# Attention and two MLPs on one core: block pairs, weight conversion and query transposes moved

## The chip, the cores and the metric

The kernel runs on one core of one Trainium2 chip. The metric is the device time of one execution in microseconds (us); a time is the median over runs. The core has five engines that run their own instruction streams in order and wait for each other by semaphores: TensorE (PE in the profile, its weight loads PEld), VectorE (DVE), ScalarE (ACT), GpSimd (POOL) and SyncE (SP), which here issues nearly all DMAs.

## The reference

Three stages, all in float32, over 4608 tokens (8 batches of 576) of width 512 (8 heads of 64):

```python
# attention, per batch and head
q_s = exp(q - max(q, -1)); q_s /= sum(q_s, -1) + 1e-09      # softmax over the 64 features
k_s = exp(k - max(k, seq)); k_s /= sum(k_s, seq) + 1e-09    # softmax over the 576 tokens
kv  = einsum('bhsd,bhse->bhde', k_s, v)
x   = einsum('bhsd,bhde->bhse', q_s, kv)                    # then (4608, 512)
# first MLP: w_in 512 x 2048, w_out 2048 x 512
h = x @ w_in;  y = (h * clip(h + 3, 0, 6) / 6) @ w_out
# second MLP, the same shapes
h = y @ w2_in; out = (h * sigmoid(h)) @ w2_out
```

## The kernel before

Tokens go in 9 blocks of 512 (`NB`). A matmul operand in float32 is held as a high part and a rest, both in the matmul's own rounded format (`F32R`), and each product is three matmuls of 128x128 weights on 512 columns (high by high, high by rest, rest by high). Weights are converted to this form by bit operations (`Conv`: `scale` and `scale_low` on ACT; `shift`, `round`, `sign` on DVE; `upper` on ACT; `lower` on DVE or POOL).

A block can be done in two ways. In the **plain** way (`mm1`, `gate`, `mm2`), a block takes 16 steps of 24 matmuls, 384 in all. In the **pair** way two blocks are multiplied together by a scheme of 7 instead of 8 products of half-size blocks (Strassen's in Winograd's form). A pair is one *pass*, with an inner half (input weights; `inner`, eight rounds `n` of the products P1, P6, P5, P2, P7, P3 and, two slots into the next round, P4) and an outer half (output weights; `outer`, 56 products). Each product is one slot of 6 matmuls, so a pass is 112 slots and 672 matmuls. It needs sums of weight parts, split into high part and rest, which lie in DRAM (`ws`), and it reads them through a ring of six buffers, two parts a fetch.

The program runs in this order:

- `first_block()` (to about 140 us): the attention of block 0 and part of the following ones, conversion of the first MLP's weights, and block 0 of the first MLP in the plain way.
- `middle()` (to about 716 us): plain blocks 1 to 6 of the first MLP (`NCL` is 7 plain blocks with block 0), and beside them the attention for the blocks to come, in *units* `u` of one block and two heads; the conversion of the second MLP's weights (`Parts`, 16 of them: 8 of `w2_in`, then 8 of `w2_out`), and the weight sums of the first MLP (`Resident`). A planner (`Plan`) writes out the order on each engine from assumed durations, keys (`begin`, `WORK`, `FETCH`, in steps) and counts of buffers.
- `second_mlp()`: five passes in the order of `PASSES`: (1, 1), (0, 7), (1, 3), (1, 5), (1, 7), where the first number is the MLP and the second the first block of the pair; then block 0 of the second MLP in the plain way. Here the order on each engine is that of the slot times given to `when`, sorted. A pass starts at slot 112 b.

In a unit of the attention, POOL and DVE normalize the queries into the one buffer `qe`. Units up to `DIRECT` (9, so all up to block 2's first) are then turned by four TensorE transposes (`q_turn`, line 476) and copied out by ACT (`q_copy`). Later units are turned by DVE in 32x32 blocks (`q_blocks`, line 484), stored to DRAM and loaded back in the right order (`q_store`, `q_load`, five DMAs).

Steps that the prediction follows in the code: in `pair_events`, `u2` and `u3` are DVE sums that read a PSUM bank before P7 and P4 may add to it, and `s5` is ACT's copy before P3; `t1` and `t2` are POOL differences of two gate outputs; `split` and `split_low` (lines 1469 to 1475) make the high part and the rest of an operand of `outer` four slots (`LOOK`) before its use; `x_ahead` makes the next pass's input operands in the outer half; `joins` adds up the results. `add` (line 1352) is the helper that records sums under line 1353.

Of the kernel before, what the change touches and what calls it, by code (L numbers as in the profile page):

```python
# [18 lines left out]
P = 128  # L19
# [9 lines left out]
def efficient_attention_then_two_mlps(  # L29
# [42 lines left out]
    ident = const.tile([P, P], F32, name="ident")  # L72
    minus = att.tile([P, DM], F32R, tag="sp", bufs=3, name="minus")[:, 0:P]
    peaks = const.tile([P, P], F32, name="peaks")
    kvt = [const.tile([P, P], F32, name=f"kv{i}") for i in range(KVS)]
# [95 lines left out]
    NPR = NF // 2  # L171
    HALF = DM // 2
# [844 lines left out]
    def middle():  # L1017

        DIRECT = 2 * NP + 1
# [5 lines left out]
        n_k, n_q, n_v, qsub, ksub, kvmm, xmm, vlow, xready = ({} for _ in range(9))  # L1025
# [4 lines left out]
        def unit(u):  # L1030
# [20 lines left out]
            if has_k and not old:  # L1051
                km = add(
                    "DVE", 1.1, key(0), lambda: k_max(u), [n_k.get(u)], ["m1", "t2k"], ["t2k"], True
# [12 lines left out]
            if has_k:  # L1066
# [3 lines left out]
                    [kx, n_v.get(u), xmm.get(u - 1)], ["a"], ["ke"],  # L1070
                )
                va = add("DVE", 0.45, key(4), lambda: kv_sum(u), [mm])
                vlow[u] = add("ACT", 0.55, key(4), lambda: kv_scale(u), [va], [], ["a"])
# [12 lines left out]
            xs_ = dma(0.35, key(6), lambda: x_store(u), 256, [xc], [], ["t2k"])  # L1086
            if j < NCL:
# [17 lines left out]
        for k in range(2 * NPR):  # L1105
            o, i = divmod(k, NPR)
            at = NF + 5.5 * k + 6 + WORK[k]
            p, done = Parts(i, o), []
            for n, c in enumerate(p.conv):
# [11 lines left out]
            for m, fn in enumerate(p.total):  # L1121
                done = [add("POOL", 0.68, at + 1.3, fn, done, [], [], True)]
            for n in range(2):
# [104 lines left out]
    def raw_x(to, j, h):  # L1228
        nc.sync.dma_start(to, yd[j, 2 * h : 2 * h + 2].rearrange("c p n -> p c n"))
# [35 lines left out]
    def first_operands():  # L1265

        def start():
            op["spare"] = xs.tile([P, 8, BLK], F32, tag="x", name="spare")
            x_steps(1)["b12"]()
# [7 lines left out]
        def load(name):  # L1277
            def do():
                operand(name, 1)
                x_steps(1)[name.lower()]()  # L1280
# [7 lines left out]
        for n, name in enumerate(("B22", "B11", "B21")):  # L1288
            jobs.append((name.lower(), "SP", 0.35, 2.5 + n, load(name), 512, ("r1",), ["wi"], False))

        def total(name, key, deps):
            jobs.append((name, "POOL", 2.1, key, lambda: x_steps(1)[name](), 0, deps, [], True))
# [42 lines left out]
    def second_mlp(last):  # L1335
        fixed = []
        for t in (kbuf[0], vbuf[0], kbuf[1], vbuf[1]):
            flat = t.rearrange("p a b c -> p (a b c)")
            fixed.append(flat[:, 0:BLK])
        for _ in range(2):  # L1340
            t = raw.tile([P, 2, BLK], F32, tag="raw", name="fin")
            fixed += [t[:, 0], t[:, 1]]
# [218 lines left out]

        turned = []
# [26 lines left out]
        def turn_last(j, k):  # L1589
# [11 lines left out]
            for i in range(4):  # L1601
# [4 lines left out]
                )  # L1606

# [140 lines left out]
```

## Time and profile before

| | |
|---|---|
| time, median of 3 runs | 1572.56 us (1572.24 to 1572.74) |
| the profiled execution: its time, its span | 1573.41 us, 1571.7 us |
| PE busy | 1557.0 us, 99% of the span, 7403 matmuls |
| DVE, ACT, POOL busy | 71%, 48%, 31% |
| TensorE clock granted | full from the first slices on |
| DMA | 342.81 MB, mean 218 GB/s |

How to read the profile: times are from one execution taken by the hardware profiler. Busy time is the union of an engine's instructions, so an instruction's own duration (mean ns) is longer than the time it takes from its engine's stream where instructions overlap. L559 is line 559 of the kernel. "<-" separates what is written from what is read; an idle time is put down to what ended it.

### The profile page before, as it was taken

The numbers are of one execution on the slowest core, as the hardware profiler recorded it, in microseconds if no ns is written. First come the engines' busy times: TensorE is split into PE (matmuls) and PEld (weight loads), VectorE is DVE, ScalarE is ACT, GpSimd is POOL, SyncE is SP. The second block draws the span as 40 slices with busy tenths as digits, with TensorE's granted clock in tenths as the row PEclk, the third lists the DMA queues.
The fourth block names the chain that finished last, engine by engine and source line by source line (L and its number), as shares of the span: only waits on it lengthen the run. The fifth ranks groups of instructions, "written<-read, shape, count | busy, mean of one in ns | idle before, by whom it ended". The sixth has DMA issues, their size and how long they took to land.

```text
span 1571.7 us, 22243 instructions
## 1 busy us (share of the span) xinstructions
PE 1557.0 (99%) x7403; PEld 1272.4 (81%) x7403; DVE 1115.9 (71%) x1791; ACT 761.0 (48%) x1358; POOL 489.2 (31%) x446
## 2 busy tenths in 40 slices
PE   7999999999999999999999999999999999999999
PEld 4787878888888888888888888888888888888887
DVE  7989577776777776555689569856976797677732
ACT  6887345554555544443365236533643464345422
POOL 4334224433434335421232242234223422440000
PEclk9999999999999999999999999999999999999999
DMA  9915976776786855746566786765668875879850
GB/s 280 335 44 176 334 227 209 238 231 203 226 257 212 264 193 189 234 152 208 189 223 217 209 233 219 260 206 198 228 213 213 224 247 194 227 224 372 260 129 27
DMA packets 346226, 342.81 MB, mean 218 GB/s; under 512 B 126464, under 2 KB 252160, under 8 KB 346112
## 3 DMA queue, kind: packets, MB, share of 16 engines
q1 hardware_dynamic: 344496, 340.70, 68.3%
q8 instruction: 59, 0.97, 0.3%
q10 hardware_dynamic: 1616, 0.69, 0.2%
q14 instruction: 55, 0.45, 0.1%
HBM read 247.20 MB, written 94.11 MB: 217 GB/s over the span
## 4 chain that ended last, share of the span: by engine, by line
PE 95%; DVE 2%; ACT 1%; DMA 1%; POOL 1%; issue 0%; SPq 0%; DVEq 0%; ACTq 0%; POOLq 0%
PE pb L1366 24%; PE pb L1525 24%; PE h L559 21%; PE y L634 19%; PE y L636 3%; PE pa L513 2%; PE pa L412 1%; DVE fa L140 0%; PE pa L384 0%; DMA ahead<-in_q_dram 0%; DMA qraw<-in_q_dram 0%; DMA wi_early<-in_moe_w_in_dram 0%; PE pa L476 0%; PE busy L875 0%; PE pa L372 0%
## 5 line engine op out<-in xcount | busy, mean ns | idle before, releaser
L559 PE MATMUL h<-x,wi 128*128 128x512 f32 x1536 | 381.8, 396 | 2.0 <-POOL wi L165 0.9
L1366 PE MATMUL pb<-xo,ring 128*128 128x512 f32 x1680 | 383.0, 389 | 0.0
L1525 PE MATMUL pb<-gsp,ring 128*128 128x512 f32 x1680 | 382.4, 389 | 0.0
L1366 PEld LDWEIGHTS pb<-xo,ring 128*128 128x128 f32 x1680 | 315.3, 188 | 65.9 <-issue 0.5
L1525 PEld LDWEIGHTS pb<-gsp,ring 128*128 128x128 f32 x1680 | 315.3, 188 | 65.5
L559 PEld LDWEIGHTS h<-x,wi 128*128 128x128 f32 x1536 | 283.2, 188 | 65.2 <-POOL wi L165 1.9
L634 PE MATMUL y<-g,wo 128*128 128x512 f32 x1344 | 323.6, 390 | 0.0
L634 PEld LDWEIGHTS y<-g,wo 128*128 128x128 f32 x1344 | 251.3, 188 | 52.7
L1353 DVE TENSOR_TENSOR gsp<-g,gsp 128x512 fp32r<-128x512 f32 x240 | 184.4, 788 | 25.0 <-ACT gsp L1471 24.2
L1471 ACT CAST gsp<-g 128x512 fp32r<-128x512 f32 x240 | 143.6, 622 | 105.4 <-PE pb L1525 89.1
L599 DVE SCALAR_TENSOR_TENSOR h<-r,h 128x512 f32<-128x512 f32 x112 | 77.7, 693 | 108.4 <-ACT r L572 108.2
L572 ACT ACTIVATE r<-h 128x512 f32<-128x512 f32 x112 | 66.9, 597 | 175.1 <-PE h L559 173.2
L1353 POOL TENSOR_TENSOR xst<-xst 128x512 f32<-128x512 f32 x32 | 70.8, 2212 | 168.6 <-DVE xo L1353 84.5
L1353 DVE TENSOR_TENSOR g<-r,pb 128x512 f32<-128x512 f32 x96 | 65.7, 684 | 54.6 <-ACT r L1380 54.1
L1380 ACT ACTIVATE r<-pb 128x512 f32<-128x512 f32 x96 | 57.1, 595 | 97.2 <-DVE pb L1353 72.8
L1353 POOL TENSOR_TENSOR g<-g 128x512 f32<-128x512 f32 x40 | 53.5, 1337 | 148.6 <-DVE g L1353 123.4
L1353 POOL TENSOR_TENSOR s<-U,s 128x512 f32<-128x512 f32 x32 | 42.6, 1330 | 173.3 <-DVE U L1353 173.3
L590 ACT CAST g<-h 128x512 fp32r<-128x512 f32 x112 | 65.5, 585 | 48.8 <-DVE h L599 40.6
L593 DVE TENSOR_TENSOR g<-h,g 128x512 fp32r<-128x512 f32 x97 | 66.8, 689 | 28.6 <-ACT g L590 26.5
L1353 DVE TENSOR_TENSOR U<-pb,s 128x512 f32<-128x512 f32 x80 | 55.0, 688 | 17.0 <-PE pb L1366 12.5
L195 POOL TENSOR_TENSOR fa<-fa 128x256 f32<-128x256 f32 x64 | 49.9, 780 | 40.7 <-DVE sp L227 32.2
L1380 ACT ACTIVATE r<-s 128x512 f32<-128x512 f32 x32 | 20.2, 632 | 87.3 <-POOL s L1353 70.3
(160 smaller groups left out, 1751.4 us busy)
## 6 DMA issues: line engine op xcount, KB each, us to landing
ring<-ws SPq DMA_DIRECT2D x280, 512.0 KB, 3.9
ws<-sp SPq DMA_DIRECT2D x128, 256.0 KB, 3.2
wi_early<-in_moe_w_in_dram SPq DMA_DIRECT2D x16, 512.0 KB, 8.5
wo_early<-in_moe_w_out_dram SPq DMA_DIRECT2D x16, 512.0 KB, 9.2
wi_raw<-in_moe_w_in_dram SPq DMA_DIRECT2D x16, 512.0 KB, 4.7
ws<-w_sum SPq DMA_DIRECT2D x32, 256.0 KB, 3.1
ws<-fa SPq DMA_DIRECT2D x32, 256.0 KB, 2.8
wo_raw<-in_moe_w_out_dram SPq DMA_DIRECT2D x16, 512.0 KB, 4.4
```

Of the source, the lines that this page charges most:

```text
L195: lambda to=to, x=x, y=y, op=op: nc.gpsimd.tensor_tensor(out=at[to], in0=at[x], in1=at[y], op=op)
L559: nc.tensor.matmul(h, w[:, a, c, :], x[:, e, c, :], start=(c == 0 and n == 0), stop=(c == NC - 1 and n == 2),)
L572: nc.scalar.activation(self.r, self.h, AF.Relu, bias=3.0)
L590: nc.scalar.copy(self.g[:, 0], self.r)
L593: nc.vector.tensor_tensor(out=self.g[:, 1], in0=self.r, in1=f32(self.g[:, 0]), op=ALU.subtract)
L599: nc.vector.scalar_tensor_tensor(out=self.h, in0=self.r, scalar=6.0, in1=self.h, op0=ALU.min, op1=ALU.mult)
L634: nc.tensor.matmul(y[c], w[:, a, cs], g[:, e, :], start=st, stop=sp)
L1353: (eng or nc.vector).tensor_tensor(out=out, in0=a, in1=b, op=how)
L1366: nc.tensor.matmul(to, ws_[:, a], e[:, c], start=p in ("P1", "P6", "P5") and c == 0 and m == 0, stop=c == 1 and m == 2, skip_group_check=True,
L1380: nc.scalar.activation(r, d[b, n, key], AF.Sigmoid)
L1471: nc.scalar.copy(t[0], source(p, i))
L1525: nc.tensor.matmul(d[b, p][m], w[:, a, m * P : (m + 1) * P], t[e], start=new and i == 0 and k == 0, stop=i == NPR - 1 and k == 2, skip_gro ...
```

## The change

Blocks 5 and 6 join blocks 7 and 8 of the first MLP as a pair (`NCL` 5 instead of 7), and both pairs are the first passes. The middle has four plain blocks instead of six, and its keys are drawn together. The eight `Parts` of `w2_out` leave the middle (`PARTS` is 8) and are made by a new function, `late_part`, inside the inner halves of the first three passes; it has the same operations as `Parts` but for POOL, in buffers that are free there. All queries are turned by TensorE (`DIRECT` 36 instead of 9). The first pass's input operands come from the attention's store `xq` instead of the first MLP's `yd`. The key-value buffers become six, and small constants are laid into common tiles.

```diff
-    KVS = NP + 1
-    NCL = NB - 2
+    KVS = NP + 2
+    NCL = NB - 4
-    PASSES = ((1, 1), (0, NCL)) + tuple((1, j) for j in range(3, NB, 2))
+    PASSES = ((0, NCL), (0, NCL + 2)) + tuple((1, j) for j in range(1, NB, 2))
...
+    PARTS = 2 * NPR - 8
...
-        m2 = tmp.tile([P, 8, D], F32, tag="t2k", name="m2")[:, 0:4]
-        m2 = m2.rearrange("p (h a) d -> p h a d", h=2)
+        m2 = halved.rearrange("p (h j d) -> p h j d", h=2, j=2)
...
-            begin[j * NP + pr] = 3 * pr if j == 1 else NF - 3 + int(3.3 * n) + LATE[n]
+            begin[j * NP + pr] = 3 * pr if j == 1 else NF - 3 + int(2.0 * n) + LATE[n]
...
-        DIRECT = 2 * NP + 1
+        DIRECT = NB * NP
...
-                qt_ = add("PE", 0.65, key(3), lambda: q_turn(u), [qn], ["a"], ["qe"])
-                ql = add("ACT", 0.62, key(3), lambda: q_copy(u), [qt_], ["qT"], ["a"])
+                qt_ = add("PE", 0.65, key(3), lambda: q_turn(u), [qn], ["a", "qT"], ["qe"])
+                ql = add("ACT", 0.62, key(3), lambda: q_copy(u), [qt_], [], ["a"])
...
-            at = NF + 5.5 * k + 6 + WORK[k]
+            at = NF + 3.4 * k + 6 + WORK[k]
-            for n, c in enumerate(p.conv):
+            for n, c in enumerate(p.conv if k < PARTS else ()):
...
-                m = None
+                m = free.get(n - 1)
...
-        nc.sync.dma_start(to, yd[j, 2 * h : 2 * h + 2].rearrange("c p n -> p c n"))
+        nc.sync.dma_start(to, xq[j - FAR, 2 * h : 2 * h + 2].rearrange("c p n -> p c n"))
...
+        words = [
+            t.rearrange("p a n -> p (a n)").bitcast(U32).rearrange("p (f t) -> p f t", t=2) for t in fin[::-1]
+        ]
+        sums = [[basis, kvs[:, 0:BLK]], [v0, kvs[:, 0:BLK]]]
+        pieces = [(kvs[:, BLK : 2 * BLK], k1), (v1, k0)]
+
+        def late_part(i, t, odd):
+            a = sums[odd]
+            rows = [2 * i, 2 * i + 1]
+            def load(n):
+                nc.sync.dma_start(
+                    words[n].rearrange("p f t -> p (f t)"),
+                    w_src[1][1][rows[n] * P : (rows[n] + 1) * P, :].bitcast(U32),
+                )
+            def scale(n):
+                nc.scalar.mul(a[n], words[n][:, :, 1].bitcast(F32), 2.0**-112)
+                nc.scalar.mul(words[n][:, :, 0], words[n][:, :, 0], 2.0**-29)
+            def bits(n):
+                au = a[n].bitcast(U32)
+                nc.vector.tensor_scalar(
+                    out=au, in0=au, scalar1=3, scalar2=None, op0=ALU.logical_shift_left
+                )
+                nc.vector.tensor_tensor(out=au, in0=au, in1=words[n][:, :, 0], op=ALU.add)
+                nc.vector.scalar_tensor_tensor(
+                    out=au, in0=words[n][:, :, 1], scalar=0x80000000, in1=au,
+                    op0=ALU.bitwise_and, op1=ALU.bitwise_or,
+                )
+            def upper(n):
+                nc.scalar.copy(pieces[n][0].bitcast(F32R), a[n])
+            def lower(n, keep):
+                hi, lo = pieces[n]
+                add((lo if keep else a[n]).bitcast(F32R), a[n], hi, ALU.subtract)
+            def store(n, keep):
+                part = Split(1, 1, i, None, NAMES[1][n] if keep else [INTO[x] for x in NAMES[1][n]], keep)
+                part.hi, part.lo = pieces[n][0], pieces[n][1] if keep else a[n]
+                part.store()
+            total = sums_in_place(1, a)
+            for n in range(2):
+                when(t - 7 + 2 * n, lambda n=n: load(n))
+                when(t + 2.2 * n, lambda n=n: scale(n))
+                when(t + 1 + 2.4 * n, lambda n=n: bits(n))
+                for k, at in enumerate((t + 3.2 + 2 * n, t + 11 + 0.6 * n)):
+                    when(at, lambda n=n: upper(n))
+                    when(at + 1 + 0.2 * k * n, lambda n=n, k=k: lower(n, not k))
+                    when(at + 2.2 + 0.2 * k * n, lambda n=n, k=k: store(n, not k))
+            for m in range(4):
+                when(t + 7.6 + 0.7 * m, total[m])
...
+        for i, t in enumerate((9, 29, 49, 121, 141, 161, 233, 250)):
+            late_part(i, t, i % 2)
```

## Rows read from the trace of the kernel before

**Rows 1.** The page, part 1: busy time, share of the span, instructions.
```profile
PE 1557.0 (99%) x7403; PEld 1272.4 (81%) x7403; DVE 1115.9 (71%) x1791; ACT 761.0 (48%) x1358; POOL 489.2 (31%) x446
```

**Rows 2.** The page, part 4: the chain that ended last, by engine.
```profile
PE 95%; DVE 2%; ACT 1%; DMA 1%; POOL 1%; issue 0%; SPq 0%; DVEq 0%; ACTq 0%; POOLq 0%
```

**Rows 3.** The page, part 5: matmuls of a plain block and of the inner halves.
```profile
L559 PE MATMUL h<-x,wi 128*128 128x512 f32 x1536 | 381.8, 396 | 2.0 <-POOL wi L165 0.9
L1366 PE MATMUL pb<-xo,ring 128*128 128x512 f32 x1680 | 383.0, 389 | 0.0
L634 PE MATMUL y<-g,wo 128*128 128x512 f32 x1344 | 323.6, 390 | 0.0
```

**Rows 4.** Stretches: length, busy PE, PEld, DVE, ACT, POOL, clock, DMA share, GB/s.
```profile
28.70:140.00 111.30, 108.16 (x543) 84.38 (x544) 101.33 (x182) 94.70 (x177) 36.83 (x32) 1.00 0.53 174
140.00:716.00 576.00, 575.33 (x2966) 469.25 (x2964) 396.92 (x688) 279.27 (x506) 221.65 (x245) 1.00 0.71 226
1071.30:1080.80 9.50, 9.50 (x43) 7.88 (x42) 5.44 (x8) 3.32 (x7) 3.87 (x3) 1.00 0.61 208
1090.30:1099.90 9.60, 9.60 (x44) 7.93 (x43) 7.33 (x11) 5.09 (x10) 3.34 (x3) 1.00 0.65 209
1099.90:1109.40 9.50, 9.50 (x44) 7.86 (x43) 9.35 (x14) 6.58 (x12) 4.64 (x4) 1.00 0.70 260
1405.00:1481.00 76.00, 76.00 (x337) 62.94 (x336) 58.09 (x87) 39.69 (x65) 3.70 (x3) 1.00 0.92 324
```

**Rows 5.** The chain in order of time: an unbroken stretch of matmuls.
```profile
796.74 74.80 PE pb L1525 x330
```

**Rows 6.** PE's timeline around one query transpose in the first block.
```profile
109.98 0.60 PE L476 MATMUL pa<-ident,qe 128*128 128x128 f32 x4
110.34 1.64 PE L559 MATMUL h<-x,wi 128*128 128x512 f32 x6
111.82 2.00 PE L634 MATMUL y<-g,wo 128*128 128x512 f32 x8
```

**Rows 7.** What PE waited for, total, times, longest: the query transposes.
```profile
PE pa L476 <- POOL qe L468: 0.5, 2, 0.3
```

**Rows 8.** Groups of DVE instructions: busy us, mean ns, idle time before.
```profile
L599 DVE SCALAR_TENSOR_TENSOR h<-r,h 128x512 f32<-128x512 f32 x112 | 77.7, 693 | 108.4 <-ACT r L572 108.2
L593 DVE TENSOR_TENSOR g<-h,g 128x512 fp32r<-128x512 f32 x97 | 66.8, 689 | 28.6 <-ACT g L590 26.5 <-PE y L634 0.7
L133 DVE TENSOR_SCALAR fa<-fa 128x512 uint32<-128x512 uint32 x64 | 35.5, 555 | 2.0 <-ACT fa L121 1.9
L140 DVE CUSTOM_DVE_ANT_0 fa<-fa,fr 128x1024 uint16<-128x1024 uint16 x64 | 51.4, 804 | 3.3
L144 DVE SCALAR_TENSOR_TENSOR fa<-wo_raw,fa 128x512 uint32<-128x512 uint32 x16 | 12.6, 790 | 0.3
L227 DVE TENSOR_TENSOR fa<-fa,sp 128x512 fp32r<-128x512 f32 x32 | 23.7, 747 | 0.6 <-ACT sp L224 0.6
L484 DVE STREAM_TRANSPOSE qz<-qe 128x512 f32<-128x512 f32 x27 | 19.0, 704 | 0.7 <-POOL qe L468 0.7
```

**Rows 9.** DVE's timeline at the end of the third pass's inner half.
```profile
1091.96 0.69 DVE L1353 TENSOR_TENSOR U<-pb,s 128x512 f32<-128x512 f32 x1
1093.86 1.35 DVE L1353 TENSOR_TENSOR gsp<-g,gsp 128x512 fp32r<-128x512 f32 x1
1097.11 0.69 DVE L1353 TENSOR_TENSOR gsp<-g,gsp 128x512 fp32r<-128x512 f32 x1 [1.30 <-ACT gsp L1471]
1098.32 0.68 DVE L1353 TENSOR_TENSOR U<-pb,s 128x512 f32<-128x512 f32 x1
```

**Rows 10.** POOL's timeline in the same stretch.
```profile
1092.01 1.29 POOL L1353 TENSOR_TENSOR g<-g 128x512 f32<-128x512 f32 x1 [2.06 <-DVE g L1353]
1093.37 1.29 POOL L1353 TENSOR_TENSOR spare<-g,g 128x512 f32<-128x512 f32 x1
```

**Rows 11.** PE's timeline there: the last round's P4.
```profile
1099.85 1.52 PE L1366 MATMUL pb<-xo,ring 128*128 128x512 f32 x6
```

More of the change, by code (lines that the diff above doesn't have):

```diff
@@ L70, in efficient_attention_then_two_mlps @@
     ps_a = ctx.enter_context(tc.tile_pool(name="ps_a", bufs=2, space=PSUM))
-    ident = const.tile([P, P], F32, name="ident")
+    basis = const.tile([P, 4 * P], F32, name="basis")
+    ident, peaks, halved = basis[:, 0:P], basis[:, P : 2 * P], basis[:, 2 * P :]
     minus = att.tile([P, DM], F32R, tag="sp", bufs=3, name="minus")[:, 0:P]
-    peaks = const.tile([P, P], F32, name="peaks")
-    kvt = [const.tile([P, P], F32, name=f"kv{i}") for i in range(KVS)]
+    kvs = const.tile([P, 2 * BLK], F32, name="kvs")
+    kvt = [kvs[:, i * P : (i + 1) * P] for i in range(KVS)]
     vbufs = const.tile([P, 2, KCH + 1, 2, D + 1], F32, name="vbuf")
@@ L1024, in middle @@
         add = plan.add
-        n_k, n_q, n_v, qsub, ksub, kvmm, xmm, vlow, xready = ({} for _ in range(9))
+        n_k, n_q, n_v, qsub, ksub, kvmm, xmm, vlow, xready, xstored = ({} for _ in range(10))
         def dma(us, key, fn, kb, deps=(), take=(), give=()):
@@ L1052, in unit @@
                 km = add(
-                    "DVE", 1.1, key(0), lambda: k_max(u), [n_k.get(u)], ["m1", "t2k"], ["t2k"], True
+                    "DVE", 1.1, key(0), lambda: k_max(u), [n_k.get(u)], ["m1"]
                 )
@@ L1069, in unit @@
                     "PE", 0.48, key(4), lambda: kv_mm(u, a_pool),
-                    [kx, n_v.get(u), xmm.get(u - 1)], ["a"], ["ke"],
+                    [kx, n_v.get(u)], ["a"], ["ke"],
                 )
-                va = add("DVE", 0.45, key(4), lambda: kv_sum(u), [mm])
-                vlow[u] = add("ACT", 0.55, key(4), lambda: kv_scale(u), [va], [], ["a"])
+                va = add("DVE", 0.45, key(4), lambda: kv_sum(u), [mm, vlow.get(u - 2)])
+                vlow[u] = add("ACT", 0.55, key(4), lambda: kv_scale(u), [va, xmm.get(u - KVS + NP)], [], ["a"])
             xm = xmm[u] = add(
@@ L1086, in unit @@
             xs_ = dma(0.35, key(6), lambda: x_store(u), 256, [xc], [], ["t2k"])
+            xstored[j, pr] = xs_
             if j < NCL:
@@ L1120, in middle @@
                 done.append(parted(p.split[n], at + n + 0.2, [c3]))
-            for m, fn in enumerate(p.total):
+            for m, fn in enumerate(p.total if k < PARTS else ()):
                 done = [add("POOL", 0.68, at + 1.3, fn, done, [], [], True)]
-            for n in range(2):
+            for n in range(2 if k < PARTS else 0):
                 parted(p.split[2 + n], at + 1.4 + n, done, ["t2k"])
@@ L1181, in middle @@
             deps = [pair_at[d] for d in deps] + [free[base + int(key)]]
+            if at[0] == "b":
+                deps += [xstored[NCL + int(at[2]) - 1, 2 * int(at[1]) - 2 + n] for n in range(2)]
             if eng == "SP":
@@ L1268, in start @@
             op["spare"] = xs.tile([P, 8, BLK], F32, tag="x", name="spare")
[L1269 removed]
+            x_steps(NCL)["b12"]()
         def get(f):
@@ L1279, in do @@
                 operand(name, 1)
-                x_steps(1)[name.lower()]()
+                x_steps(NCL)[name.lower()]()
             return do
@@ L1288, in first_operands @@
         for n, name in enumerate(("B22", "B11", "B21")):
-            jobs.append((name.lower(), "SP", 0.35, 2.5 + n, load(name), 512, ("r1",), ["wi"], False))
+            jobs.append((name.lower(), "SP", 0.35, 2.5 + n, load(name), 512, ("r1", "b12"), ["wi"], False))
         def total(name, key, deps):
-            jobs.append((name, "POOL", 2.1, key, lambda: x_steps(1)[name](), 0, deps, [], True))
+            jobs.append((name, "POOL", 2.1, key, lambda: x_steps(NCL)[name](), 0, deps, [], True))
         def split(name, key, deps):
@@ L1335, in second_mlp @@
     def second_mlp(last):
[L1336 to L1342, printed above, removed]
+        k0, v0, k1, v1 = (
+            t.rearrange("p a b c -> p (a b c)")[:, 0:BLK] for t in (kbuf[0], vbuf[0], kbuf[1], vbuf[1])
+        )
+        fin = [raw.tile([P, 2, BLK], F32, tag="raw", name="fin") for _ in range(2)]
+        fixed = [
+            x for m, (one, three) in enumerate(((k0, k1), (v0, v1)))
+            for x in (one, fin[0][:, m], three, fin[1][:, m])
+        ]
         whole = xs.tile([P, 4, 2, DM], F32R, tag="x", name="ring")
```

5 lines of the change are left out of this document (3 added, 2 removed).

## The prediction, made before the run

> **What bounds the kernel now.** I read the page's busy times first, then the chain, then the stretches, then the places where the change puts work. TensorE is busy for 99% of the span [rows 1], and the chain that ended last is 95% PE [rows 2]. The reader should see that nothing else sets the end: between 140 and 716 us, where the change takes out two blocks, PE idles 0.67 us of 576 although DVE is busy for 69% of it [rows 4]. Only the first block shows idle time, 3.14 us of 111.3, with DVE at 91% [rows 4]. So the time changes by what PE's own stream loses and gains, plus any wait that the change newly puts on PE. DVE's load matters only as a source of such waits.
>
> The unit price is that of one matmul in an unbroken stretch: 330 of them take 74.80 us, 0.2267 us each, and a slot of six 1.36 us [rows 5]. The durations of 389 to 396 ns in [rows 3] overlap and are not a price.
>
> **The pair.** A plain block has 192 matmuls at line 559 and 192 at line 634: 1536 and 1344 are eight and seven times 192, the eighth being the second MLP's plain block [rows 3]. A pass has 1680/5 = 336 inner and as many outer [rows 3], so 672. Two plain blocks have 768. The change takes away 96 matmuls: 96 x 0.2267 = **21.8 us off**. This is certain as far as the counts go. The order of the passes costs PE nothing by itself: blocks 5 and 6 reach `xq` from the attention about seven steps before the first pass reads them by the keys, and the pass with blocks 1 and 2 now comes third.
>
> **The query transposes.** 27 units get four TensorE transposes each. In the first block they begin at 109.98 and the next matmul at 110.34, so the four take 0.36 us of starts; the six matmuls behind take 1.48 us instead of 1.36, since the weights after a transpose load late [rows 6]. One unit alone costs 0.36 + 0.12 = 0.48 us. Where the transposes stand next to other attention work that late load is paid already, so 0.36 is the lower bound. I take 0.44, because both cases occur: 27 x 0.44 = **11.9 us added** (9.7 to 13.0). What they replace lay on no path: 27 DVE transposes, 19.0 us [rows 8], and 135 DMAs on SP's queue. The 27 copies by ACT go beside; ACT is busy for 48% of the middle [rows 4].
>
> A page of the Trainium skill would make this part a loss. "TensorE: Matmul & The Clock Gate", Part 4, gives about 275 ns for a transpose in a kernel; 27 x 4 x 0.275 is an estimate of 29.7 us, and the change would come out near 1588.6 us. The trace decides: four of them take 0.36 to 0.48 us together here [rows 6].
>
> **The shorter middle.** It loses 32 steps (174.1 us) and gains 11.9, so 414 us remain of 576. DVE loses 32 x (0.69 + 0.69) = 44 us of gates, 16 conversions of 0.56 + 0.80 + 0.79 + 2 x 0.75 = 3.65 us, 58 us, and the 19.0 us of transposes [rows 8]: 397 - 121 = 276 us, or 67% of the new length against 69%. Attention and `w2_in` lie mostly in the first two thirds, so DVE is nearer to the first block's 91% there than the mean says. Moving the keys together shortens each unit's distance to the next; buffers `qe` and `qT` are single, and `q_turn` must now wait for `qT` until the former unit's `x_mm` has run. Behind a PE instruction that waits stand all later matmuls, so a late query stops PE, which a late DVE transpose did not. Row: nine units cost 0.5 us of waiting for POOL's normalization [rows 7]; 27 give 1.5. Bounds: nothing (the old middle), and the first block's idle rate over 414 us, 3.14/111.3 x 414 = 11.7 us [rows 4]. I take **1.5 us added**, nearer to the old middle, whose mean DVE load is the new one's.
>
> **The late weights in the passes.** Each of the eight late parts puts on DVE two times `bits` (0.56 + 0.80 + 0.79) and four rests of 0.75, 7.3 us in all [rows 8], within 14 slots (19 us). A round of an inner half is 7 slots, and DVE is busy for 5.44 of its 9.5 us [rows 4], so two rounds leave 8.1 us. Parts that begin at slot 9, 26 or 29 of a pass fit: **0.6 us** for the six (0 to 3). ACT has more room, 3.32 of 9.5 us busy [rows 4]. In DMA a part brings 1 MB in and 2 MB out within 20 slots, 27 us, some 115 GB/s on top of 208; the last outer half moved 324 GB/s while PE was unbroken [rows 4], so I cost it at nothing. Its cover is the ring, twelve slots ahead; SP's stores wait for DVE's rests, and the fetches behind them wait too.
>
> The parts at slot 49 of the first and second pass (t = 49 and 161) do not fit. Their first DVE work falls into slots 50 to 56, where DVE also makes the first operands of the outer half: 7.33 of 9.6 us busy, 2.3 idle [rows 4]. Ahead of the last round's `u3` stand both `bits` and one rest, 5.05 us, so `u3` is 2.75 us late. It ended at 1099.00 and P4 began at 1099.85 [rows 9, 11]: the slack is 0.85, and PE waits 1.9 us. The next slice has 0.15 us of DVE idle [rows 4], so the other three rests, 2.2 us, are passed on; operands made four slots ahead absorb perhaps half, and 1.1 us is left. A tail costs 3.0 us, bounds 1.0 (most of it absorbed) and 4.9 (7.3 less all idle time). Two tails: **6.0 us added** (2 to 9.8).
>
> POOL makes this worse. A DVE rest that met POOL's `t2` took 1.35 us and ended 0.5 us after it; the one 3 us later took 0.69 [rows 9, 10]. A late part's DVE work meets `t1` and `t2` in the same way. The Trainium skill, "SBUF — State Buffer", section "Who interferes with whom", says that a DVE instruction with two SBUF inputs and a GpSimd one that reads SBUF lock each other out for the whole instruction; that speaks against work placed here, and the trace agrees. Without such a lock I should put a tail at 1.8 instead of 3.0 us and the whole 2.4 us lower.
>
> **Sum.** -21.8 + 11.9 + 1.5 + 0.6 + 6.0 = -1.8 us. Against the profiled execution (1573.41 us, span 1571.7, 1.7 us outside) that is 1571.6; this execution is 0.85 us over the median, and the median 1572.56 gives **1570.8 us**. A measurement can tell 0.2% here, 3.1 us, so the forecast is no measurable change; its own range, from the tails' 4 to 8 us and the middle's 0 to 3, is 1567 to 1574.
>
> **Rivals.**
> - *The cover holds.* Tails and middle together cost up to 5 us. For it: `outer` makes its operands four slots ahead, and in slots 56 to 63 DVE already runs at 98% without stopping PE [rows 4]. Against it: `u3` has 0.85 us of slack and no such lead. -9.9 + (0 to 5) gives 1562.7 to 1567.7.
> - *The middle becomes DVE's.* Queries and keys reach PE late at the first block's rate from the first unit on: 11.7 us, in all -9.9 + 6.6 + 11.7 = +8.4, 1581.0 us. It decides as soon as all waits exceed 13 us. For it: the packed first two thirds and single `qe` and `qT`. Against it: the old middle waited 0.67 us.
> - *The ring starves* in the first inner halves. The late traffic comes in bursts, with the stores blocking SP; a wait of 2 to 4 us in each of the first two passes gives about 1577. Against it: 324 GB/s with PE unbroken [rows 4].
> - *The transposes do not overlap* with what follows and cost their whole 0.60 us [rows 6]: 16.2 instead of 11.9, 1575.1 us; the page cited above points there. The start times speak against it.
>
> **How the numbers follow.** Forecast 0.42, cover holds 0.33, middle 0.17, ring 0.05, transposes 0.03. About a fifth of the forecast's cases lie under 1569.4 and count as faster: 0.33 + 0.08 = 0.41 faster; 0.36 the same, with a few mild cases of the rivals; the rest slower, 0.23. The range leaves out the far ends of the first two rivals: 1563 to 1580.
>
> **What would show it.** Matmuls at lines of the inner and outer halves must be 2016 each, and PE's busy time falls by about 10 us. Right: PE's idle time after 28 us grows by some 8 us, of which the greater part is P4 waiting for `u3`, and the outer half's first products waiting for DVE rests, in passes one and two near their slots 50 to 66; the third pass shows none. The query transposes wait 1 to 2 us for POOL in all. Wrong: unbroken matmuls through both places (the cover holds), idle time spread over the middle before PE's attention work (the middle), or matmuls waiting for ring fetches. A transposed unit that costs over 0.5 us would make the second term wrong.

## The result, and the profile after

The changed kernel takes **1591.05 us** (median of 4 runs, 1589.22 to 1591.73), the kernel before 1572.52 beside it: ratio 1.0116, interval 1.0099 to 1.0134. It is 18.5 us slower, and the forecast of 1570.8 us with its range of 1563 to 1580 missed it. The profiled execution of after took 1589.22 us, 1.8 us under its median, with a span of 1587.0 us; the sums below are made against the span of before, 1571.7 us, which leaves 15.3 us to explain (the execution of before lay 0.9 us over its median).

The page of after, part 1 (answers [rows 1]) and the matmul groups of part 5 (answers [rows 3]; us busy, mean ns, idle time before the group):

```profile
PE 1557.7 (98%) x7415; PEld 1263.1 (80%) x7415; DVE 1183.1 (75%) x1849; ACT 799.7 (50%) x1433; POOL 549.8 (35%) x478
...
L1370 PE MATMUL pb<-xo,ring 128*128 128x512 f32 x2016 | 463.8, 390 | 11.8 <-ACT s L1410 6.4
L1529 PE MATMUL pb<-gsp,ring 128*128 128x512 f32 x2016 | 462.1, 390 | 2.7 <-DVE gsp L1357 2.5
L559 PE MATMUL h<-x,wi 128*128 128x512 f32 x1152 | 293.9, 399 | 1.8 <-POOL wi L166 0.9
L634 PE MATMUL y<-g,wo 128*128 128x512 f32 x960 | 235.0, 393 | 0.0
```

The counts are those foreseen: 2016 matmuls in the inner halves and as many in the outer. What is new is the third column: the inner halves had no idle time ahead of their matmuls before, now 11.8 us, and the outer halves now have 2.7.

What PE waited for in after (total us, times, longest), the lines that concern the change:

```profile
PE pb L1370 <- ACT s L1410: 6.4, 5, 2.3
PE pb L1370 <- DVE U L1357: 5.1, 4, 1.5
PE pb L1529 <- DVE gsp L1357: 2.5, 4, 0.9
PE pa L384 <- ACT kvs L429: 1.8, 1, 1.8
PE pa L513 <- DVE ke L393: 1.0, 1, 1.0
PE pa L476 <- POOL qe L468: 0.8, 3, 0.3
```

L1410 is `s5`, ACT's copy ahead of P3; `U` at L1357 is `u2` or `u3` on DVE, ahead of P7 and P4; `gsp` is the rest of an operand of the outer half.

The end of the middle and the first four passes of after (stretch, length, busy PE, PEld, DVE, ACT, POOL, clock, DMA share, GB/s):

```profile
422.00:556.60 134.60, 134.60 (x657) 108.53 (x657) 84.45 (x128) 68.35 (x118) 65.82 (x66) 1.00 0.53 176
556.60:719.00 162.40, 158.11 (x685) 127.60 (x684) 137.51 (x201) 84.31 (x150) 51.89 (x36) 1.00 0.81 275
719.00:882.20 163.20, 156.57 (x674) 125.10 (x673) 134.54 (x191) 82.71 (x148) 62.41 (x44) 1.00 0.79 264
882.20:1039.00 156.80, 153.23 (x674) 125.89 (x673) 128.51 (x181) 79.67 (x141) 57.70 (x40) 1.00 0.73 245
1039.00:1191.30 152.30, 152.30 (x674) 126.11 (x673) 116.34 (x169) 69.68 (x124) 49.96 (x32) 1.00 0.74 221
```

The fourth pass is unbroken, 152.3 us, 672 x 0.2267. The three passes with late parts take 162.4, 163.2 and 156.8 us. The first contains 2.7 us of other matmuls; by the starts of PE's matmuls the rest over 152.3 us is 7.4, 10.8 and 4.5 us, 22.6 in all, and comes from waiting. With these starts the span's 15.3 us divide so:

| | predicted us | read in after |
|---|---|---|
| two plain blocks replaced by a pass | -21.8 | -21.8 (32 steps of 5.44, a pass of 152.3) |
| 27 query transposes | +11.9 | +12.4 (27 x 0.46) |
| waits in the middle | +1.5 | +2.3 |
| late parts at slots 9, 26, 29 | +0.6 | +9.7 |
| late parts at slot 49, two tails | +6.0 | +13.0 (5.9 and 7.1) |
| a wait in the first pass of before, now gone | 0 | -0.4 |
| sum | -1.8 | +15.2 |

The two terms of the late parts are the sums, slot by slot, of what the starts of six matmuls are apart beyond 6 x 0.2267 us. Tails are slots 53 to 70; the early parts show at P3 of rounds 2 and 4 above all. What a wait costs in starts is more than the idle time that the profile shows for it: the 2.26 us of idle time in the next section cost 2.5 us, because idle time counts from the end of the matmul before (0.39 us long) and not from the start that was due 0.23 us behind it, and because the second matmul after the wait comes 0.11 us late as well. Of the 22.6 us only 14.5 (11.8 and 2.7) are listed as idle. In what follows "waits" of whole passes are counted by the starts, and single waits ahead of one product by idle time unless the text says otherwise.

**How one wait comes about.** The third pass has no tail, and its longest wait, ahead of round 4's P3, is 2.26 us. PE, ACT, DVE and POOL there in after (start, us, engine, line, operation):

```profile
931.38 1.89 PE L1370 MATMUL pb<-xo,ring 128*128 128x512 f32 x7 [2.26 <-ACT s L1410]
...
930.26 0.60 ACT L1384 ACTIVATE r<-pb 128x512 f32<-128x512 f32 x1 [3.39 <-DVE pb L1357]
930.75 0.58 ACT L1410 COPY s<-pb 128x512 f32<-128x512 f32 x1
...
925.39 0.69 DVE L1357 TENSOR_TENSOR U<-pb,s 128x512 f32<-128x512 f32 x1
925.99 1.14 DVE L1589 TENSOR_SCALAR kvs<-kvs 128x512 uint32<-128x512 uint32 x1
927.26 1.57 DVE L1592 CUSTOM_DVE_ANT_0 kvs<-fin,kvs 128x1024 uint16<-128x1024 uint16 x1
928.87 0.69 DVE L1593 SCALAR_TENSOR_TENSOR kvs<-fin,kvs 128x512 uint32<-128x512 uint32 x1
929.48 0.69 DVE L1357 TENSOR_TENSOR pb<-s,pb 128x512 f32<-128x512 f32 x1
...
925.56 1.30 POOL L1357 TENSOR_TENSOR g<-g 128x512 f32<-128x512 f32 x1 [3.38 <-DVE g L1357]
926.93 1.35 POOL L1357 TENSOR_TENSOR spare<-g,g 128x512 f32<-128x512 f32 x1
```

Read it upwards. POOL makes `t1` and `t2` from 925.56 to 928.28. Beside them the late part's shift takes 1.14 us and its round 1.57, each ending 0.3 to 0.55 us after a POOL operation; sign, behind both, takes 0.69. So the three end 3.5 us after `u2`, where undisturbed they take 1.8. Only then comes `c21` (929.48), then ACT's activation of the former round, which waits for it, and behind that, on ACT's in-order stream, `s5`. PE's P3 waits for `s5`. The wait is named after ACT, ACT had idled 3.39 us, and the cause is on DVE and POOL.

**The tail.** DVE, POOL, ACT and PE of the second pass of after, at the end of its inner half:

```profile
792.56 1.58 DVE L1592 CUSTOM_DVE_ANT_0 vbuf<-fin,vbuf 128x1024 uint16<-128x1024 uint16 x1
794.17 1.66 DVE L1593 SCALAR_TENSOR_TENSOR vbuf<-fin,vbuf 128x512 uint32<-128x512 uint32 x1
795.76 0.68 DVE L1357 TENSOR_TENSOR U<-pb,s 128x512 f32<-128x512 f32 x1
...
809.13 1.63 POOL L1357 TENSOR_TENSOR spare<-g,g 128x512 f32<-128x512 f32 x1
810.72 1.19 POOL L197 TENSOR_TENSOR vbuf<-vbuf 128x256 f32<-128x256 f32 x1
811.98 1.07 POOL L197 TENSOR_TENSOR vbuf<-kvs,vbuf 128x256 f32<-128x256 f32 x1
...
813.09 0.62 ACT L1599 CAST kvs<-vbuf 128x512 fp32r<-128x512 f32 x1 [2.87 <-POOL vbuf L197]
...
796.49 3.42 PE L1370 MATMUL pb<-xo,ring 128*128 128x512 f32 x12 [1.54 <-DVE U L1357]
802.70 1.65 PE L1370 MATMUL pb<-xo,ring 128*128 128x512 f32 x6 [1.43 <-DVE U L1357]
815.71 9.12 PE L1529 MATMUL pb<-gsp,ring 128*128 128x512 f32 x36 [0.93 <-DVE gsp L1357]
```

P7 waits for `u2` behind round and sign, P4 for `u3`, and the outer half's slot 64 for a rest. The last comes by a way that the prediction didn't have: POOL makes most of the part's totals (L197) only after `t2`, ACT's `upper` (L1599) waits 2.87 us for them, and ACT's high parts of the outer operands stand behind it.

### The profile page after: what moved, and what is told of

Read it like the earlier page. It is cut to its first block, busy times and chain, and to the rows that moved or that the text cites. A ratio compares the mean times of both kernels' runs of the same rounds, so it can differ in the third digit from the quotient of the medians.

```text
span 1587.0 us, 22379 instructions
## 1 busy us (share of the span) xinstructions
PE 1557.7 (98%) x7415; PEld 1263.1 (80%) x7415; DVE 1183.1 (75%) x1849; ACT 799.7 (50%) x1433; POOL 549.8 (35%) x478
## 5 line engine op out<-in xcount | busy, mean ns | idle before, releaser
L1370 PE MATMUL pb<-xo,ring 128*128 128x512 f32 x2016 | 463.8, 390 | 11.8 <-ACT s L1410 6.4
L1529 PE MATMUL pb<-gsp,ring 128*128 128x512 f32 x2016 | 462.1, 390 | 2.7 <-DVE gsp L1357 2.5
L1370 PEld LDWEIGHTS pb<-xo,ring 128*128 128x128 f32 x2016 | 377.0, 188 | 96.7 <-ACT s L1410 10.7
L1529 PEld LDWEIGHTS pb<-gsp,ring 128*128 128x128 f32 x2016 | 377.7, 188 | 85.2 <-DVE gsp L1357 6.1
L559 PE MATMUL h<-x,wi 128*128 128x512 f32 x1152 | 293.9, 399 | 1.8 <-POOL wi L166 0.9
L559 PEld LDWEIGHTS h<-x,wi 128*128 128x128 f32 x1152 | 210.8, 188 | 48.2 <-POOL wi L166 1.9
L1357 DVE TENSOR_TENSOR gsp<-g,gsp 128x512 fp32r<-128x512 f32 x288 | 222.9, 792 | 25.8 <-ACT gsp L1475 25.1
L634 PE MATMUL y<-g,wo 128*128 128x512 f32 x960 | 235.0, 393 | 0.0
L634 PEld LDWEIGHTS y<-g,wo 128*128 128x128 f32 x960 | 178.5, 188 | 37.2
L1357 POOL TENSOR_TENSOR xst<-xst 128x512 f32<-128x512 f32 x40 | 92.7, 2318 | 202.1 <-DVE xo L1357 114.0
L1357 POOL TENSOR_TENSOR s<-U,s 128x512 f32<-128x512 f32 x40 | 53.7, 1341 | 207.1 <-DVE U L1357 199.6
L1357 POOL TENSOR_TENSOR g<-g 128x512 f32<-128x512 f32 x48 | 65.6, 1367 | 154.7 <-DVE g L1393 87.5
L1357 DVE TENSOR_TENSOR g<-r,pb 128x512 f32<-128x512 f32 x96 | 65.6, 683 | 44.8 <-ACT r L1384 43.8
L1357 DVE TENSOR_TENSOR U<-pb,s 128x512 f32<-128x512 f32 x96 | 65.8, 686 | 14.3 <-PE pb L1370 10.7
L1357 POOL TENSOR_TENSOR spare<-g,g 128x512 f32<-128x512 f32 x48 | 66.2, 1379 | 3.8
```

The lines of the kernel that those rows point to most:

```text
L559: nc.tensor.matmul(h, w[:, a, c, :], x[:, e, c, :], start=(c == 0 and n == 0), stop=(c == NC - 1 and n == 2),)
L634: nc.tensor.matmul(y[c], w[:, a, cs], g[:, e, :], start=st, stop=sp)
L1357: (eng or nc.vector).tensor_tensor(out=out, in0=a, in1=b, op=how)
L1370: nc.tensor.matmul(to, ws_[:, a], e[:, c], start=p in ("P1", "P6", "P5") and c == 0 and m == 0, stop=c == 1 and m == 2, skip_group_check=True,
L1529: nc.tensor.matmul(d[b, p][m], w[:, a, m * P : (m + 1) * P], t[e], start=new and i == 0 and k == 0, stop=i == NPR - 1 and k == 2, skip_gro ...
```

## The experiments

The theory at the start was the order on the engines: in an inner half DVE, ACT and POOL pass a round's values around in program order, and late work delays them. Its rivals were the late DMA traffic, the choice of how queries are turned, the choice of where the weights are converted, and, within the theory, whether one wait or one engine is to blame.

### Late parts without their arithmetic

```diff
-                when(t + 2.2 * n, lambda n=n: scale(n))
-                when(t + 1 + 2.4 * n, lambda n=n: bits(n))
...
-                    when(at, lambda n=n: upper(n))
-                    when(at + 1 + 0.2 * k * n, lambda n=n, k=k: lower(n, not k))
-                    when(at + 2.2 + 0.2 * k * n, lambda n=n, k=k: store(n, not k))
-            for m in range(4):
-                when(t + 7.6 + 0.7 * m, total[m])
+                    when(at + 2.2 + 0.2 * k * n, lambda n=n, k=k: store_raw(n, not k))
```

> Of the eight late parts only the DMAs stay (512 KB loads, 256 KB stores from a constant tile); their work on ACT, DVE and POOL is left out, so the second MLP's output weights are not made. In the changed kernel the first three passes last 162.4, 163.1 and 156.8 us where an unbroken pass is 152.3 (the first with 2.7 us of other matmuls in it). Theory A, the waits come from the late parts' work in the in-order queues of DVE and ACT: the passes fall to about 155.0, 152.3 and 152.3 us, the span from 1587.0 to about 1565. Rival B, the traffic delays the ring's fetches or the next pass's operands: the passes stay over 156 us and the span stays over 1580.

1565.69 us (1565.68 to 1567.15), ratio 0.9959, interval 0.9943 to 0.9974. The first three passes of this kernel:

```profile
557.70:712.70 155.00, 155.00 (x685) 128.39 (x684) 118.51 (x171) 72.61 (x126) 39.12 (x24) 1.00 0.84 288
712.70:865.00 152.30, 152.30 (x673) 126.17 (x672) 111.23 (x161) 69.92 (x124) 50.05 (x32) 1.00 0.83 283
865.00:1017.30 152.30, 152.30 (x673) 126.16 (x672) 111.57 (x161) 70.82 (x125) 50.30 (x32) 1.00 0.73 252
```

PE is never idle although the transfers are all there, at 252 to 288 GB/s. So DMA costs nothing, as predicted, and all 22.6 us come from the arithmetic. (The stores here need not wait for DVE's rests; but in after, too, no wait of PE is put down to a ring fetch.) The kernel also gives the net of the other terms: its span is 1565.4 us, 6.3 under before, where -21.8 + 12.4 + 2.3 makes -7.1. Its passes begin 1.1 us later than those of after, 557.7 against 556.6 us; its middle has 3.4 us, from 228.9 us on, at a granted clock of 0.50, which the profiled execution of after doesn't have.

### `s5` ahead of the activations

```diff
-            when(e["P5"] + 0.1, s5)
+            when(e["P5"] - 0.4, s5)
```

> One key is changed: ACT's copy s5 is issued ahead of the sigmoid or relu of the former round's last product, instead of behind it. Theory A1, P3 waits because s5 stands on ACT behind that activation, which waits for DVE's sum of s1 and P4's bank, which stands behind the late parts' bit operations: the waits before P3 in the inner halves (about 1.0, 3.2 and 4.1 us in passes 1 to 3, and 0.8 us in the two tails) go, and the passes fall to about 160.5, 159.5 and 152.5 us, span about 1578. Rival A2, DVE is simply short of time in these stretches, so that another of its results is late instead: P7, P4 or the outer half's first products wait for what P3 waited before and the span stays within 2 us of 1587.

1587.85 us (1587.25 to 1588.30), ratio 1.0096 (1.0081 to 1.0111). The waits of P3 in rounds 2 and 4 are gone. In their place P4 of round 4 waits 0.5, 1.6 and 1.6 us (by the starts) for `u3` in the three passes, and the tails keep their price. The passes wait 20.1 us instead of 22.6, so only some 2.5 us come back: `s5` was the first value to be late, not the only one.

### Queries of units 12 to 35 turned by DVE and DRAM again

```diff
-        DIRECT = NB * NP
+        DIRECT = 12
```

> Units 12 to 35 have their queries turned by DVE and DRAM again, as in the kernel before; only units 9 to 11 of the added ones stay with TensorE. Theory A, a unit's four transposes cost PE 0.46 us and the middle hides the other way: 24 x 0.46 = 11 us less in the middle (422.5 us to about 411), span about 1576, passes as in the changed kernel. Rival C, the shortened middle can't hide the way through DRAM: PE waits before its attention products, or attention runs out beyond the last plain step, and the middle gains less than 6 us or gets longer.

1595.84 us (1594.48 to 1596.09), ratio 1.0145 (1.0130 to 1.0160). Three new waits of PE:

```profile
PE pb L1370 <- DMA ring<-ws: 4.4, 1, 4.4
PE y L634 <- ACT g L590: 2.6, 2, 2.1
PE pa L513 <- ACT kvs L429: 2.4, 1, 2.4
```

24 units, some 11 us of transposes, are saved, but the middle is only 1.5 us shorter (421.0 against 422.5), so some 9.6 us return; and the first pass then waits 4.4 us for its ring. Not all of that is waiting. In the middle PE's idle time grows by 5.2 us, from 3.2 to 8.4. Behind waits, from 368.0 and from 528.4 us, two stretches of 3.4 us have a granted clock of 0.50, which is the lower level, 1.2 GHz; from 566.0 us, within the wait for the ring, 6.8 us have it, and the slots behind that wait take up to 2.70 us instead of 1.36. In this order of the middle the way over DVE and DRAM gains nothing, so here the 12.4 us are part of the price of removing two blocks from it. The waits named are for ACT, though, for gates and for the key-value part; how the turning of the queries leads to them was not followed.

### All 16 conversions of the second MLP in the middle

```diff
-    PARTS = 2 * NPR - 8
+    PARTS = 2 * NPR
...
-        for i, t in enumerate((9, 29, 49, 121, 141, 161, 233, 250)):
-            late_part(i, t, i % 2)
```

> All sixteen conversions stay in the middle and no late part is made; pair order and query transposes are as in the changed kernel. Theory A: passes 1 to 3 are 155.0, 152.3 and 152.3 us, and the middle, with DVE at about 80% of its 422 us, waits little more (0 to 5 us): span 1565 to 1570. Rival C, the middle was too full for them: it grows by 10 us or more and the span is 1575 or above.

1651.79 us (1651.05 to 1652.11), ratio 1.0502 (1.0484 to 1.0519). Its largest wait of PE:

```profile
PE pb L1370 <- ACT s L1404: 72.4, 1, 72.4
```

The stretches behind its last plain steps (columns as above):

```profile
540.00:560.00 20.00, 18.10 (x78) 13.94 (x77) 17.08 (x21) 11.35 (x21) 9.62 (x9) 1.00 0.50 164
560.00:580.00 20.00, 9.33 (x42) 7.37 (x40) 12.33 (x19) 8.90 (x15) 4.48 (x6) 0.82 0.78 243
580.00:600.00 20.00, 0.00 (x0) 0.00 (x0) 10.57 (x17) 8.72 (x15) 4.41 (x6) 0.50 0.81 276
```

The conversions run on for some 70 us after the middle's matmuls are through, with PE idle and DVE at half load: what they lack there is not DVE's capacity. Of ACT's waits between 575 and 640 us 29.1 are for DMAs (loads of the raw weights, and stores that make buffers free) and 12.5 for POOL's totals; what orders them was not followed further. The second and third pass are unbroken at 152.3 us. So with these keys and buffers the weights could not stay where they were either; another order of the middle was not tried.

### The late parts in every other round, in buffers of their own

```diff
-        for i, t in enumerate((9, 29, 49, 121, 141, 161, 233, 250)):
-            late_part(i, t, i % 2)
+        for i in range(8):
+            b, m = divmod(i, 3)
+            late_part(i, 112 * b + 14 * m - 1, m % 2)
```

with `bits` put where POOL should be idle, and the second splitting in buffers that hold nothing else.

> The late parts have the same operations, DMAs and passes, but other places: a part begins at round 0, 2 or 4 of an inner half, one of its two conversions in each round, with the bit operations between the round's gate product after P4 and u3, where POOL has no t1, t2 or c22 under way in the traces; the second split comes two rounds later in its own buffers; nothing stands in the last round. Theory A (place in the in-order queues and the shared stretches with POOL): waits of passes 1 to 3 fall from 22.2 us to under 4, span 1565.5 to 1569, a time under the kernel before by 4 us or more. Rival A2 (DVE lacks the time): each pass still waits 3 us or more, span over 1574.

1590.45 us (1588.15 to 1594.54), ratio 1.0121 (1.0103 to 1.0138): no gain. The tails are gone, but the passes take 164.1, 160.4 and 156.7 us, with waits of up to 2.7 us ahead of P2, P3 and P4. Some 1.7 us of the second pass are the clock: behind the 2.4 us wait ahead of round 4's P4 the granted clock is 0.50 for 3.4 us, and nine matmuls start 0.43 us apart instead of 0.23. One cause can be read: ACT's `scale` at 757.31 us waited 2.56 us for the store of the former part from the same buffer, and a round's `s5` stood behind it. So a spacing that suits POOL fails at another queue.

### Without `t1` and `t2`

```diff
-            when(e["P3"] + 1.9, t1)
-            when(e["P3"] + 2.0, t2)
+            if b >= 3:
+                when(e["P3"] + 1.9, t1)
+                when(e["P3"] + 2.0, t2)
```

> The late parts stand where the changed kernel has them; POOL's differences t1 and t2 are left out in the first three passes (their tiles keep other numbers). DVE, ACT and DMA have the same work. Theory L (a late part's bit operations and rests are held while POOL's t1 and t2 run): the first shift, round and sign of a part take about 0.4, 0.7 and 0.7 us instead of up to 1.2, 1.6 and 1.7, waits fall from 22.2 to about 6 to 8 us, most of it in the two tails, span about 1572. Rival O (order and DVE time alone): waits stay over 15 us, span over 1579.

1570.30 us (8 runs, 1569.29 to 1571.62), ratio 0.9986 (0.9976 to 0.9997). The waits fall from 22.6 to 3.5 us, the tails from 13.0 to 2.0. 2.7 us of POOL work a round decide over nearly all of it, although not one of DVE's or ACT's operations is gone.

### Only the two parts at slot 49

```diff
+            if t not in (49, 161):
+                for n in range(2):
+                    when(t - 7 + 2 * n, lambda n=n: load(n))
+                    for k, at in enumerate((t + 3.2 + 2 * n, t + 11 + 0.6 * n)):
+                        when(at + 2.2 + 0.2 * k * n, lambda n=n, k=k: store_raw(n, not k))
+                return
```

> Only the two parts at slot 49 of passes 1 and 2 do their work; the other six keep their DMAs alone, so their weights are not made. Theory T (a tail has its own price): passes 1 and 2 wait 5.5 to 7.5 us each as at slots 53 to 70 in the changed kernel, pass 3 nothing, span about 1578. The price of the prediction, 3.0 us a tail, gives 1571.4. Rival: the six earlier parts leave DVE behind and the tails only inherit it; then the two tails cost under 4 us each.

1577.31 us (1576.31 to 1578.40), ratio 1.0028 (1.0014 to 1.0041). The tails cost 4.9 and 6.0 us and the third pass nothing. That is a tail's price by itself, 5.4 us where the prediction had 3.0; with the earlier parts at work it is 5.9 and 7.1.

### Parts and differences moved together, and the differences alone

```diff
+            later = ({0: 17.0, 1: 20.1, 2: 32.1, 3: 35.1, 4: 47.1, 5: 50.1, 6: 52.0}, {0: 17.0, 1: 20.1, 2: 32.1, 3: 35.1})
...
-            late_part(i, t, i % 2)
+            b, m = divmod(i, 3)
+            late_part(i, 112 * b + 15 * m + 7, m % 2)
```

> The changed kernel with two moves: late parts begin at slots 7, 22, 37 of the first two passes and 7, 22 of the third, so that none reaches into the first operands of the outer half with its bit operations; and POOL's differences t1 and t2 of rounds 0 to 6 of these passes are issued later, into stretches where no late part has bit operations or rests. The same operations are done. Theory L (the late work is held by POOL's t1 and t2): waits of passes 1 to 3 fall from 22.2 to 3 to 6 us, span 1568 to 1571, a time 1.5 to 4 us under the kernel before. Rival (place alone was wrong, t1 and t2 matter little): the tails' 12 us go and 8 to 10 us stay, span 1573 to 1575. Rival (moving t1 and t2 makes other work late): more than 10 us stay.

1583.99 us (1582.47 to 1584.93), ratio 1.0070 (1.0058 to 1.0082). What PE waited for in this kernel's inner halves:

```profile
PE pb L1370 <- ACT s L1410: 5.7, 5, 1.6
PE pb L1370 <- DVE U L1357: 2.1, 4, 0.8
PE pb L1370 <- ACT s L1404: 1.5, 4, 0.5
```

The waits of the outer half are gone and those for `u2` and `u3` more than halved, but about 17 us of waits remain. It is the best arrangement tried, still 11 us slower than before. The second kernel leaves the parts where the change has them and only starts `t1` and `t2` later:

```diff
+            later = ({0: 19.1, 1: 22.6, 2: 24.6, 3: 39.1, 4: 42.6, 5: 44.6, 6: 56.1}, {0: 19.1, 1: 22.6, 2: 24.0, 3: 36.1, 4: 40.0})
```

> Only the keys of t1 and t2 in the first three passes are changed (later, outside the late parts' bit operations and rests); late parts stay at the slots of the change. Theory L: the earlier six parts wait about 1 us in all instead of 9.5, the two tails 3 to 4 us each instead of 6.4; span about 1572 to 1574. Rival O (the order in DVE's and ACT's queues, not POOL, makes the waits): span stays within 3 us of 1587.

1588.61 us (1588.11 to 1590.19), ratio 1.0101 (1.0088 to 1.0114), which the interval does not tell from the change; the waits are 22.1 us. This is what the rival expected. New waits, of 0.5 to 1.1 us by the starts, stand ahead of round 3's P7, where `c22` is now queued behind the moved differences on POOL and holds up ACT's activation and copies. What is moved out of one value's way stands in the next one's.

### The differences on DVE

```diff
-                add(g[:, 1], g[:, 1], g[:, 0], ALU.subtract, nc.gpsimd)
+                add(g[:, 1], g[:, 1], g[:, 0], ALU.subtract, nc.vector if b < 3 else nc.gpsimd)
```

and `t2` likewise.

> t1 and t2 of the first three passes are done by DVE instead of POOL, at the same keys; DVE gets about 1.2 us more in each round of 9.5 us, POOL 2.6 us less. Theory L: DVE has more work and yet the waits fall, since its operations on two tiles of SBUF are held less: from 22.2 to 8 to 14 us, span 1573 to 1579. Rival A2 (DVE lacks the time): the waits grow to 30 us or more, span over 1594.

1597.32 us (1596.45 to 1598.36), ratio 1.0155 (1.0141 to 1.0168). Its two largest waits of PE:

```profile
PE pb L1370 <- DVE U L1357: 10.5, 11, 1.7
PE pb L1370 <- ACT s L1410: 6.9, 6, 2.0
```

`t1` and `t2` disturb DVE no longer: all sixteen shifts of the late parts take 0.42 to 0.43 us, and 1.57 us are left to three rounds of sixteen, beside `c22`. Yet PE waits about 31 us in the three passes. DVE doesn't have the time for `t1` and `t2` as well, short as they are on it. This leaves open how much of the price in the changed kernel is the disturbance of DVE by POOL, and how much POOL's own queue; the last experiment divides them as far as it goes.

### Fills in place of the differences

```diff
+                if b < 3:
+                    for _ in range(3):
+                        nc.gpsimd.memset(g[:, 1], 0.0)
+                    return
```

and in `t2` the same on `op["spare"][:, n]`.

> In the first three passes the differences t1 and t2 on POOL are replaced by three fills with zero each, of the same 128x512 tiles and at the same places (so these two operands of the outer half hold zeros). A fill of 128x2048 took 1.81 us elsewhere, so three of 128x512 should take about 1.3 to 1.5 us, as one difference does: POOL's stream is as long as in the changed kernel, and c22 and the totals still stand behind it, but nothing is read from SBUF by POOL. Theory L (the late part's DVE operations are held up by POOL's reads, and that makes the waits): shift, round and sign beside t1 and t2 go back to 0.42 to 0.69 us, the waits of the three passes fall from 22 us to the 4 us seen where t1 and t2 were left out, and the time is 1569 to 1573 us. Rival Q (POOL's own queue: c22, and the totals that ACT waits for, come late behind t1 and t2 whatever they do): the DVE operations shorten but the waits stay at 15 us or more, 1582 to 1590 us. In between, the share of the 18 us that comes back is the share of the lock.

1580.28 us (1579.44 to 1582.22), ratio 1.0048 (1.0032 to 1.0065): between the two. DVE and POOL at the place shown above, round 4 of the third pass:

```profile
914.19 1.58 DVE L1600 CUSTOM_DVE_ANT_0 vbuf<-fin,vbuf 128x1024 uint16<-128x1024 uint16 x1
...
919.03 0.42 DVE L1597 TENSOR_SCALAR kvs<-kvs 128x512 uint32<-128x512 uint32 x1
919.58 0.69 DVE L1600 CUSTOM_DVE_ANT_0 kvs<-fin,kvs 128x1024 uint16<-128x1024 uint16 x1
...
913.88 1.34 POOL L1357 TENSOR_TENSOR s<-U,s 128x512 f32<-128x512 f32 x1 [1.99 <-DVE U L1357]
918.58 1.92 POOL L1442 MEMSET g<- 128x512 f32 x3 [3.36 <-DVE g L1357]
```

Beside POOL's fills shift and round take 0.42 and 0.69 us; beside `c22`, which reads, round takes 1.58 as before. The P3 behind it still waits 1.48 us for `s5`, where in the changed kernel it waits 2.26 and without `t1` and `t2` 0.62. DVE's busy time in the three passes is 383.9 us against 400.6 (the sums of three stretches): 16.6 us of it were the disturbance by `t1` and `t2`. The waits fall to 13.4 us, so 9.2 of the 19.1 us that `t1` and `t2` cost are due to the difference between subtracting and filling, and the trace shows that as DVE's delay. The other 9.9 us, 13.4 against 3.5, remain when POOL is merely occupied at these places; some of them may be DVE's delay as well, beside `c22` and the totals when these come late, which this experiment doesn't separate. Three fills take 1.6 us on the mean, 0.25 more than a difference, so this half is somewhat too large and the first too small.

## Why the prediction was wrong

**Right.** The pair, -21.8 us by the counts. The transposes: 27 at 0.46 make 12.4 us, inside the bounds. The line's own answer in after shows why a duration must not be taken for the price (count: least, median, greatest ns):

```profile
L476 PE MATMUL pa<-basis,qe x144: 270/272/418, 12.5 to 539.3; 128*128 128x128 f32 x144
```

One lasts 272 ns, but four and the late weight load behind them delay the next matmuls by 0.46 us in all. The 275 ns of the Trainium skill's "TensorE: Matmul & The Clock Gate", Part 4, agree with the duration; taken as a price they would have given an estimated 29.7 us. The 1588.6 us that the prediction drew from that lie 2.5 us from the measured time by coincidence. DMA cost nothing.

**Right by luck.** The middle's waits were 2.3 us for 1.5, but not for queries: the 0.8 us ahead of line 476 all lie before 61 us, in the first block, and the 27 units turned in the middle waited for none. PE waited for the key-value part (1.8 ahead of line 384, 1.0 ahead of line 513; before had 1.0 us of other waits in its middle, which goes off). Of the rivals listed, the second came nearest with its 1581 us, but its mechanism, a middle bound by DVE, did not occur. The ring never starved.

**Wrong: the six early parts, 0.6 against 9.7 us.** The step that failed is "DVE is busy for 5.44 of its 9.5 us, so two rounds leave 8.1 us ... fit". It set work against idle time. But DVE's idle time in a round is waiting for ACT and POOL, and theirs is waiting for DVE; what counts is how late each value may be. The margin was worked out for `u3` alone, in the tail (0.85 us [rows 9, 11]), and not for `s5`, which stands on ACT behind the activation that needs `c21`. In the third pass of before, round 4 (start, us, engine, line, operation):

```profile
1066.05 0.59 ACT L1406 COPY s<-pb 128x512 f32<-128x512 f32 x1
...
1023.69 46.63 PE L1366 MATMUL pb<-xo,ring 128*128 128x512 f32 x205
```

The pass runs unbroken from 1023.69, and P3 of round 4 is its slot 33, so it begins 198 x 0.2267 us later, at 1068.57: `s5` ended 1.9 us before P3 began, and so it does in the other rounds. `bits` takes 1.8 us undisturbed and up to 3.6 to 3.8 beside `t1` and `t2`, as shown above, so ahead of `c21` it exceeds that. (Of the sixteen `bits`, eight have a lengthened round, of about 1.57 us; three of these meet `c22`.) The experiment without `t1` and `t2` shows that busy share was no measure: DVE was at 82% there (379.7 of 463.3 us), and PE waited 3.5 us; in the changed kernel DVE is at 83% (400.6 of 482.4), and PE waited 22.6.

**Wrong in size: the tails, 3.0 against 5.4 alone and 5.9 and 7.1 in place.** The mechanism and the slots were right: `u3` late at slot 56, rests late at slots 64 to 70. Missed were P7's wait for `u2` at slot 53 (1.0 and 1.8 us by the starts), POOL's totals behind `t2`, for which ACT and with it the outer half's high parts waited, and the size of the disturbance.

The signs that the prediction named say the same. The counts held. But PE's idle time after 28 us grew by 16 us instead of 8, PE's busy time rose by 0.7 us instead of falling by 10 (part of what the waits cost is listed as busy time, see above), P4's waits for `u3` are only 2.9 us of the idle time, and the third pass, where none was expected, lost 4.5 us.

**The disturbance was known and under-priced.** The prediction read one DVE rest of 1.35 us beside `t2` [rows 9, 10] and drew 2.4 us from it in all. By the fills it is some 9 us. The rule of "SBUF — State Buffer", section "Who interferes with whom", in the Trainium skill, that the two engines lock each other out for whole instructions, agrees with the traces: 0.69 becomes 1.57 beside an operation that reads, and stays 0.69 beside fills. Shift, which has one input, is lengthened as well (0.42 becomes 1.14), and POOL's own operations grow from 1.29 to 1.63.

**Why no arrangement helped enough.** Work taken out brings the time back (1565.7 without the arithmetic, 1570.3 without `t1` and `t2`); work moved brings back 7 us at best (1584.0, 1588.6, 1590.5), and work handed to DVE none (1597.3). The three engines form one loop with little margin per round of 9.5 us, and each part adds to all three. That no hand-made order of the same work lies below 1572.5 us is not shown; the room for one is the 6.3 us that the kernel without the arithmetic leaves.

## What to carry to other kernels

Before work goes into the gaps of busy engines, follow each value that TensorE waits for back through every in-order queue, list its margin, and set the new instruction against the smallest margin behind which it is queued: idle time of engines that wait for each other is no room. Price DVE work beside a GpSimd operation that reads SBUF by the time until that operation ends (here the DVE operation ended 0.3 to 0.55 us behind it), not by its own. A block taken out of a well covered stage also takes the cover away: here 21.8 us of matmuls were exchanged for 12.4 us of transposes and 24.6 us of added waits.

## What had not been expected of the hardware

Beside GpSimd fills of the same tiles (0.54 us each on the mean) DVE's rounds and signs stayed at 0.69 us; of the sixteen shifts fourteen took 0.42 to 0.43 us, and two, beside fills, 0.52 and 0.57. A GpSimd difference lengthened even a shift, a DVE operation with one SBUF input, from 0.42 to 1.14 us. In the kernel with all conversions in the middle the granted clock fell to 0.82 and 0.50 in the stretches in which PE ran out of work, 0.50 being the lower level, 1.2 GHz; the passes behind them ran at 152.3 us again.
